# Filler matmuls on constants in five waits of TensorE, in a sliding-window attention kernel followed by a mixture of experts

## The chip, the cores and the metric

The kernel runs on one core of one Trainium2 chip. The metric is the time of one execution on the device in microseconds (us). Before the change it is the median of three runs.

## The reference

Attention over 8 batches, 8 heads, 576 positions and a head size of 64, in which a position sees the positions at a distance of at most 32; then a layer with 8 experts, of which each of the 4608 rows goes to one.

```python
scores = scale * np.matmul(q, k.transpose(0, 1, 3, 2))
mask = np.abs(pos[:, None] - pos[None, :]) <= 32
attn = softmax(np.where(mask, scores, -1e9))
x = np.matmul(attn, v)                       # -> rows of 512 = 8 heads x 64
logits = x @ w_gate + modality_bias[modality_id]
e = argmax(logits); gate = softmax(logits)[e]
out[row] = gate * (relu(x[row] @ w1[e]) @ w2[e])   # 512 -> 1024 -> 512
```

## The kernel before

All work is cut into small named operations, and one long string, `ORDER`, gives the order in which the program issues them. A token is read as a name, its numbers, after a slash the engine that copies (`a` ScalarE or ACT, `v` VectorE or DVE, `p` GpSimd or POOL), and after a colon the PSUM bank or banks into which TensorE writes. Each engine works through its own instructions in this order; semaphores make it wait for what others have to deliver. The eight PSUM banks are handed out by the string alone.

For each batch, `l` loads q or k for four heads, `c` casts them to bf16 (tile `cb`), `TQ` and `TK` transpose them on TensorE (L496), and `tq` and `tk` copy the result to `qT` and `kT`. `lr`, `cr`, `TR` (L508) and `tr` do the same for the last 64 positions. `lv` loads v, and `cv` casts it to `vt`. For batches 1 and 2 the load of v goes to the tile `vb` in another layout, and the matmuls `Y` (L283) bring it into order, with `yy` as the copy.

The attention runs in 32 steps of a batch and a pair of heads. `SA` and `SB` are the scores of key blocks 0 and 1, and of 2 to 4 (L528, two banks each). `sa` and `sb` are their exponentials on ACT (L536, L539) into the tile `pt`. `M` multiplies by the band mask on DVE (L550), `V` multiplies by v (L564, L569), and `v` normalises on DVE (L578, L579). A copy that POOL makes waits for the latest mask multiplication of DVE, by an explicit dependency. `Kd`, once, prepares the bias from the modality ids: a small transpose (L413) and eleven operations on DVE.

After each batch `X` transposes its rows (L590) and `L` computes the logits (L603). The chains `lo`, `B`, `Q` and `E` pick the expert; `R` counts the rows by a triangular matmul (L657, L659); `P` makes each row's place (its last step gives `di`). `Z` scatters the batch's rows by expert into a table in device memory, in five indirect transfers that POOL issues (L690). `F` fetches a tile of 256 rows of the table, `N` transposes it, `U` (L824) and `D` (L842) are the two expert matmuls, `u` and `y` their copies, and `O` scatters the result rows to the output (L859). `W` loads an expert's weights on POOL's queue (L732, L735).

So the first stage, in which the first batches' attention and routing run, has little for TensorE to do and many chains between engines; later, attention and the expert matmuls are interleaved and TensorE has work all the time.

The two constants that the change uses are in place early: `ident` is a 128 x 128 identity, and `mask` the band mask of 128 x 192, written by POOL (L353 to L356) between its first and its second cast.

Of the kernel before, what the change touches and what calls it, by code (L numbers as in the profile page):

```python
# [33 lines left out]
TK1:3 tk0/a TR0:4 tk1/v lv0.1 tr0.0/a SA0:56 lv0.2 tr0.1/a c0.1.0/v sa0 lv0.3 SB0:01 SA1:23 sb0 TQ2:7 SB1:45  # L34
tq2/v c0.1.1/p TQ3:6 lv0.4 sa1 tq3/v TK2:0 sb1 M0 l1.0.0 TK3:1 l1.0.1 Kd:7 tk2/a cv0.0/p lr1.0 tk3/a M1 lr1.1
cv0.1/p l1.1.0 cv0.2/a l1.1.1 V0:23 V1:45 v0 c1.0.0/p zp SA2:01 SB2:67 sa2 v1 SA3:23 sb2 c1.0.1/p SB3:01 TQ4:4
TQ5:5 lv1.0 sa3 tq4/v TK4:6 TK5:7 M2 sb3 lv1.4 tk4/v cr1/p tq5/a V2:23 M3 tk5/a TR1:4 SA4:01 tr1.0/a tr1.1/a
v2 c1.1.0/p V3:56 sa4 c1.1.1/p v3 TQ6:7 SB4:23 TQ7:4 tq6/a W0 SA5:01 sb4 tq7/v X0.0:5 X0.1:6 X0.2:7 x0.0/v
X0.3:4 x0.1/a x0.2/v X0.4:2 Y1.0:3 x0.3/a x0.4/v Y1.1:5 yy1.0/a Y1.2:6 M4 yy1.1/a L0:7 Y1.3:4 yy1.2/a lo0
SB5:23 B0.0 I0 yy1.3/a TK6:5 B0.1 TK7:7 Q0.0 sa5 B0.2 tk6/v E0 B0.3 sb5 V4:01 tk7/v SA6:45 B0.4 Q0.1 SB6:67 v4  # L40
sa6 R0:2 sb6 P0.0 Q0.2 P0.1 P0.4 P0.2 P0.5 P0.3 A0.0 Z0.0 Z0.1 Z0.2 Z0.3 Z0.4 A0.1 M5 l2.0.0 l2.0.1 lr2.0 A0.2
V5:34 M6 lr2.1 SA7:01 l2.1.0 SB7:56 sa7 A0.3 l2.1.1 v5 sb7 V6:01 A0.4 c2.0.0/p v6 F0 TQ8:2 A0.5 TQ9:7 M7 tq8/a
F1 lv2.0 tq9/a l3.0.0 c2.0.1/p V7:34 l3.0.1 v7 lr3.0 lv2.4 cr2/a TK8:5 TK9:6 lr3.1 tk8/a TR2:0 tk9/v X1.0:1
tr2.0/a X1.1:2 X1.2:7 x1.0/a tr2.1/v c2.1.0/p X1.3:3 l3.1.0 X1.4:4 x1.1/v x1.2/a SA8:56 SB8:01 x1.3/a x1.4/v
TQ10:2 TQ11:7 sa8 tq10/v L1:4 sb8 tq11/v SA9:23 SB9:56 lo1 B1.0 I1 sa9 B1.1 Q1.0 Y2.0:7 B1.2 E1 M8 Y2.1:4
yy2.0/a Y2.2:0 yy2.1/a Y2.3:1 B1.3 Q1.1 B1.4 l3.1.1 yy2.2/a Q1.2 R1:2 yy2.3/v c2.1.1/p sb9 N0:3 P1.0 P1.1
TK10:7 P1.2 TK11:4 n0/a P1.4 V8:01 P1.3 P1.5 Z1.0 tk10/v N1:5 tk11/a v8 SA10:23 U0.0:6 n1/a Z1.1 U0.1:7 u0.0/a
Z1.2 c3.0.0/v sa10 SB10:01 u0.1/v U0.2:4 Z1.3 sb10 c3.0.1/v TQ12:5 U0.3:6 Z1.4 u0.2/a tq12/v TK12:2 TQ13:3
u0.3/a W1 A1.0 TK13:7 lv3.0 M9 D0.0.0:0 tk12/a lv3.1 tq13/a lv3.2 D0.0.1 A1.1 M10 tk13/a lv3.3 Ke V9:45 y0.0/a
lv3.4 D0.1.0:1 A1.2 v9 cr3/a c3.1.0/a V10:23 A1.3 i0 SA11:67 TR3:0 A1.4 sa11 SB11:45 v10 F2 O0.0 D0.1.1 sb11  # L50
tr3.0/v l4.0.0 SA12:67 TQ14:2 A1.5 TQ15:3 tr3.1/v c3.1.1/p sa12 tq14/v SB12:45 M11 sb12 TK14:0 TK15:2 tk14/v
tq15/a V11:67 M12 tk15/a SA13:45 l4.0.1 sa13 SB13:23 v11 cv3.0/p sb13 lr4.0 y0.1/v X2.0:0 X2.1:4 X2.2:5 x2.0/a
M13 X2.3:6 F3 X2.4:7 x2.1/a x2.2/a x2.3/v O0.1 lr4.1 x2.4/a i1 L2:2 U1.0:3 lo2 B2.0 I2 B2.1 U1.1:1 Q2.0
cv3.1/p u1.0/a l4.1.0 U1.2:0 E2 u1.1/a B2.2 B2.3 Q2.1 U1.3:4 B2.4 u1.2/a Q2.2 cv3.2/p l4.1.1 R2:5 u1.3/a P2.0
V12:67 P2.1 P2.2 V13:23 P2.4 P2.3 P2.5 SA14:01 Z2.0 v12 N2:4 sa14 v13 n2/a SB14:56 Z2.1 SA15:01 sb14 SB15:23
Z2.2 c4.0.0/v lv4.0 U2.0:7 sa15 Z2.3 TQ16:4 u2.0/v U2.1:5 sb15 A2.0 TQ17:6 M14 U2.2:0 u2.1/a U2.3:1 lv4.1 A2.1
u2.2/a A2.2 tq16/v tq17/a V14:23 u2.3/v D1.0.0:7 Z2.4 c4.0.1/a v14 lv4.2 D1.0.1 A2.3 TK16:5 A2.4 y1.0/a N3:0
M15 TK17:4 n3/a D1.1.0:6 A2.5 lv4.3 tk16/v O1.0 V15:12 tk17/a cr4/v D1.1.1 v15 TR4:3 y1.1/a SA16:45 c4.1.0/p
U3.0:7 tr4.0/v lv4.4 sa16 tr4.1/v O1.1 X3.0:0 X3.1:1 u3.0/v X3.2:2 x3.0/a X3.3:6 X3.4:3 x3.1/v x3.2/a SB16:45
TQ18:7 i2 x3.3/a D2.0.0:0 x3.4/v sb16 c4.1.1/p SA17:12 tq18/v l5.0.0 L3:6 F4 TQ19:3 i3 sa17 U3.1:7 lo3 M16 I3  # L60
tq19/a SB17:45 TK18:6 u3.1/a D2.0.1 B3.0 tk18/v sb17 F5 TK19:1 B3.1 U3.2:2 B3.2 Q3.0 B3.3 E3 tk19/v D2.1.0:3
y2.0/a l5.0.1 u3.2/v U3.3:7 O2.0 cv4.0/a lr5.0 D2.1.1 u3.3/a B3.4 Q3.1 M17 R3:6 lr5.1 D3.0.0:4 y2.1/a l5.1.0
P3.0 D3.0.1 O2.1 cv4.1/a cv4.2/v D3.1.0:5 y3.0/a P3.1 l5.1.1 Q3.2 P3.2 P3.4 V16:01 P3.3 P3.5 Z3.0 c5.0.0/a
V17:23 v16 SA18:67 lv5.0 TQ20:4 sa18 D3.1.1 Z3.1 v17 tq20/a SB18:01 TQ21:6 Z3.2 y3.1/v sb18 N4:7 SA19:23
tq21/v SB19:45 Z3.3 n4/a Z3.4 sa19 U4.0:0 A3.0 sb19 lv5.1 M18 U4.1:1 U4.2:6 u4.0/a A3.1 u4.1/v O3.0 lv5.2
c5.0.1/a V18:23 u4.2/v O3.1 U4.3:7 cr5/a v18 lv5.3 TK20:4 u4.3/a TR5:5 A3.2 TK21:0 tk20/v U5.0:1 tr5.0/a
tr5.1/a lv5.4 A3.3 M19 SA20:23 tk21/a D4.0.0:6 u5.0/a SB20:45 A3.4 sa20 i4 U5.1:7 F6 A3.5 i5 sb20 c5.1.0/p
c5.1.1/v V19:01 D4.0.1 l6.0.0 u5.1/a v19 SA21:23 TQ22:4 sa21 l6.0.1 TK22:5 M20 TQ23:7 SB21:01 tq22/a TK23:2
tk22/v cv5.0/p lr6.0 X4.0:3 sb21 X4.1:4 x4.0/v X4.2:5 x4.1/a lr6.1 x4.2/v X4.3:3 X4.4:0 U5.2:1 x4.3/a M21
x4.4/a l6.1.0 D4.1.0:4 cv5.1/p cv5.2/v u5.2/a l6.1.1 L4:5 tq23/a tk23/v U5.3:3 y4.0/a lo4 B4.0 I4 F7 i6 V20:01  # L70
B4.1 u5.3/a Q4.0 O4.0 V21:56 E4 v20 SA22:23 D4.1.1 sa22 lv6.0 B4.2 Q4.1 SB22:01 B4.3 Q4.2 y4.1/a D5.0.0:7 B4.4
v21 c6.0.0/p sb22 lv6.1 SA23:23 R4:4 D5.0.1 O4.1 c6.0.1/v lv6.2 sa23 SB23:56 P4.0 TQ24:0 M22 sb23 TK24:1 lv6.3
TQ25:2 TK25:3 P4.1 tq24/a P4.2 V22:56 P4.4 lv6.4 tk24/a P4.3 P4.5 U6.0:4 A4.0 Z4.0 v22 tq25/a SA24:01 u6.0/a
U6.1:2 l7.0.0 tk25/v Z4.1 sa24 y5.0/v D5.1.0:5 u6.1/a Z4.2 cr6/v U6.2:6 c6.1.0/a A4.1 TR6:4 M23 U6.3:3 u6.2/a
tr6.0/a TQ26:0 A4.2 u6.3/a D5.1.1 Z4.3 tr6.1/v l7.0.1 tq26/a c6.1.1/v V23:12 Z4.4 y5.1/a SB24:67 v23 TK26:4
sb24 TQ27:3 O5.0 TK27:0 U7.0:5 lr7.0 tk26/v tq27/a O5.1 SA25:12 tk27/v X5.0:6 X5.1:7 u7.0/a lr7.1 X5.2:4
x5.0/v X5.3:3 x5.1/a X5.4:0 D6.0.0:5 A4.3 x5.2/a x5.3/v SB25:67 x5.4/a A4.4 M24 D6.0.1 F8 sa25 L5:3 A4.5 sb25
y6.0/v cv6.0/p U7.1:4 l7.1.0 lo5 D6.1.0:0 O6.0 cv6.1/v l7.1.1 cv6.2/a u7.1/a U7.2:1 B5.0 I5 Q5.0 B5.1 V24:23
E5 M25 lv7.0 u7.2/a U7.3:5 B5.2 Q5.1 V25:67 B5.3 u7.3/a lv7.1 B5.4 D6.1.1 Q5.2 v24 c7.0.0/p c7.0.1/a SA26:45
R5:1 lv7.2 y6.1/a v25 SB26:23 cr7/p lv7.3 sa26 O6.1 TQ28:0 P5.0 SA27:67 sb26 tq28/v SB27:45 P5.1 F9 P5.4  # L80
TK28:0 P5.2 sa27 TR7:1 P5.5 P5.3 TQ29:2 A5.0 TK29:3 M26 sb27 U8.0:6 lv7.4 A5.1 D7.0.0:7 tk28/a tr7.0/v Z5.0
u8.0/v tr7.1/a V26:45 tq29/a tk29/v Z5.1 U8.1:0 c7.1.0/a v26 SA28:12 Z5.2 D7.0.1 u8.1/a c7.1.1/v sa28 SB28:34
Z5.3 TQ30:6 U8.2:5 sb28 y7.0/v Z5.4 tq30/v TK30:0 TQ31:1 u8.2/a TK31:2 tk30/v D7.1.0:7 tq31/a A5.2 M27 tk31/a
U8.3:3 D7.1.1 A5.3 u8.3/a M28 V27:45 y7.1/a A5.4 D8.0.0:6 i7 F10 A5.5 v27 O7.0 cv7.0/a SA29:01 D8.0.1 sa29 i8
F11 SB29:23 O7.1 y8.0/a cv7.1/v X6.0:7 X6.1:4 X6.2:5 x6.0/a X6.3:0 X6.4:1 x6.1/v O8.0 U9.0:6 x6.2/a x6.3/v
x6.4/a D8.1.0:7 i9 u9.0/a cv7.2/p L6:4 sb29 i10 U9.1:5 lo6 B6.0 I6 V28:01 B6.1 u9.1/a Q6.0 B6.2 M29 U9.2:6 E6
SA30:23 U9.3:4 u9.2/a B6.3 B6.4 Q6.1 sa30 v28 R6:5 D8.1.1 u9.3/a P6.0 V29:23 Q6.2 y8.1/a P6.1 P6.4 SB30:01
P6.2 U10.0:6 P6.3 sb30 P6.5 A6.0 v29 Z6.0 SA31:45 D9.0.0:7 u10.0/a SB31:01 sa31 A6.1 U10.1:2 M30 sb31 D9.0.1
u10.1/v Z6.1 V30:34 y9.0/a A6.2 U10.2:6 M31 D9.1.0:5 u10.2/a A6.3 v30 Z6.2 V31:01 U10.3:2 Z6.3 v31 D9.1.1
u10.3/a Z6.4 X7.0:7 X7.1:6 X7.2:3 y9.1/a A6.4 x7.0/v O8.1 X7.3:4 x7.1/a X7.4:0 U11.0:1 x7.2/v x7.3/a O9.0  # L90
D10.0.0:2 u11.0/a x7.4/v F12 U11.1:5 A6.5 i11 O9.1 L7:7 u11.1/a D10.0.1 F13 lo7 B7.0 I7 U11.2:6 B7.1 Q7.0
y10.0/a B7.2 B7.3 D10.1.0:3 E7 B7.4 u11.2/a O10.0 R7:4 U11.3:0 P7.0 P7.1 Q7.1 D10.1.1 P7.2 u11.3/a Q7.2 P7.3
P7.4 i12 D11.0.0:1 y10.1/a P7.5 A7.0 Z7.0 U12.0:5 D11.0.1 u12.0/a A7.1 i13 A7.2 U12.1:7 Z7.1 y11.0/a D11.1.0:2
u12.1/a A7.3 Z7.2 U12.2:6 A7.4 Z7.3 D11.1.1 u12.2/a U12.3:4 A7.5 y11.1/a Z7.4 H0 H1 J0 D12.0.0:0 u12.3/a H2
O10.1 H3 J1 U13.0:3 H4 H5 H6 O11.0 D12.0.1 H7 u13.0/a H8 H9 U13.1:5 O11.1 y12.0/a F14 G0 G1 D12.1.0:1 G2
# [14 lines left out]
def kernel(  # L110
# [12 lines left out]
    nc = tc.nc  # L123
    B, H, S, D = q.shape
    P = 128
# [186 lines left out]
    ident = const.tile([P, P], BF16)  # L312
# [229 lines left out]
    op["SA"] = lambda _, it: scores(it, 0)  # L542
    op["SB"] = lambda _, it: scores(it, 2)
    op["sa"] = lambda _, it: exps(it, 0)
    op["sb"] = lambda _, it: exps(it, 2)

    @named
    def M(_, it):
# [550 lines left out]
```

## Time and profile before

| | before |
|---|---|
| time of three runs | 262.41, 263.61, 263.88 us, median 263.61 |
| profiled execution | span 262.5 us, mean granted TensorE clock 0.946 |
| TensorE busy | 221.5 us (84%), 2529 matmuls |
| ACT, DVE, POOL busy | 170.7, 159.5, 126.0 us (65%, 61%, 48%) |
| data moved | 52.14 MB, mean 199 GB/s |
| chain that ended last | TensorE 42%, issue 15%, POOL 8%, DVE 6%, DMA 3%, ACT 3% |

The profile is of one execution. Busy times are sums over the span and say nothing about when: TensorE's slices show four to seven tenths in the first third and nine tenths afterwards. The granted clock is the share of full speed at which TensorE may run; it has its own row of 40 slices, each 6.6 us long. "Idle before, released by" in the rows below means how long an engine stood still before an instruction, and what ended that.

### The profile page before, as it was taken

Reading aid. Unit: us, or ns where it says so; the run is one execution under the profiler, and the core shown is the slowest. Engines: PE = TensorE matmul, PEld = TensorE weight load, DVE = VectorE, ACT = ScalarE, POOL = GpSimd, SP = SyncE. Lnnn points to the kernel's source line nnn. Section 1 sums busy time; section 2 is a strip of 40 time slices with the busy share of each in tenths; the row PEclk is TensorE's granted clock in tenths of the full one; section 3 lists DMA queues with packets and bytes.
Section 4 is the critical chain, followed back from the end, with each engine's and each line's share of the span. In section 5 each row is a group of like instructions: output and inputs, shape, how many; then the busy total and the mean of one; then the engine's idle time right before and its main releaser. Section 6 shows DMA issues by size and latency. Waiting matters only on the chain.

```text
span 262.5 us, 6727 instructions
## 1 busy us (share of the span) xinstructions
PE 221.5 (84%) x2529; PEld 157.3 (60%) x2529; DVE 159.5 (61%) x463; ACT 170.7 (65%) x296; POOL 126.0 (48%) x162
## 2 busy tenths in 40 slices
PE   0736676298977999998999999999999999999960
PEld 0426535286745876666775777667677666666630
DVE  7684949459788579757887769884863815100000
ACT  2653745279886596879787996978746455555540
POOL 2937512863875275057244755644374671222240
PEclk9999975569998899999999999999999999999996
DMA  4999999599999998999499999949029559422220
GB/s 154 267 224 283 272 259 212 153 167 295 294 182 236 303 303 212 216 310 298 125 245 249 267 289 212 267 123 203 20 80 204 183 167 201 133 81 85 81 82 8
DMA packets 85523, 52.14 MB, mean 199 GB/s; under 512 B 58435, under 2 KB 81003, under 8 KB 85483
## 3 DMA queue, kind: packets, MB, share of 16 engines
q1 hardware_dynamic: 73131, 31.27, 54.2%
q0 software_dynamic: 11680, 19.84, 29.0%
q10 hardware_dynamic: 672, 0.53, 0.6%
q8 instruction: 21, 0.34, 0.6%
q14 instruction: 19, 0.16, 0.2%
HBM read 38.18 MB, written 16.11 MB: 207 GB/s over the span
## 4 chain that ended last, share of the span: by engine, by line
PE 42%; issue 15%; POOL 8%; DVE 6%; DMA 3%; ACT 3%; POOLq 1%; DVEq 0%; ACTq 0%
PE banks L824 15%; PE banks L842 13%; POOL out_dram L859 5%; PE banks L528 3%; DMA out_dram<-ys,ix 3%; PE banks L496 3%; PE banks L590 3%; PE banks L564 2%; ACT pt L536 2%; PE banks L569 2%; POOL scr L690 1%; DVE xt L579 1%; DVE pt L550 1%; PE banks L603 1%; DVE kT L191 1%
## 5 line engine op out<-in xcount | busy, mean ns | idle before, releaser
L824 PE MATMUL banks<-xTf,w 128*128 128x256 bf16 (+1 forms) x608 | 77.2, 273 | 1.0 <-ACT xTf L189 0.9
L842 PE MATMUL banks<-w,hT 128*128 128x512 bf16 x296 | 74.7, 379 | 0.0
L824 PEld LDWEIGHTS <-w 128*128 128x128 bf16 x608 | 56.9, 99 | 15.8 <-issue 1.7
L859 POOL DMA_INDIRECT out_dram<-ys,ix x37 | 37.4, 1011 | 57.4 <-ACT ys L850 31.9
L690 POOL DMA_INDIRECT scr<-xt,di x40 | 44.7, 1118 | 39.0 <-issue 37.0
L835 ACT ACTIVATE hT<-banks 128x512 bf16<-128x512 f32 x65 | 39.0, 599 | 34.8 <-PE banks L824 34.0
L536 ACT ACTIVATE pt<-banks 128x768 bf16<-128x768 f32 x64 | 50.8, 821 | 14.9 <-PE banks L528 12.0
L842 PEld LDWEIGHTS <-hT 128*128 128x128 bf16 x296 | 27.2, 98 | 21.4 <-issue 0.8
L550 DVE TENSOR_TENSOR pt<-pt,mask 128x1920 bf16<-128x1920 bf16 x32 | 38.0, 1189 | 0.3 <-ACT pt L539 0.3
L496 PE MATMUL banks<-ident,cb 128*128 128x128 bf16 x256 | 24.0, 241 | 15.0 <-POOL cb L193 14.7
L564 PE MATMUL banks<-vt,pt 128*128 128x65 bf16 x320 | 24.0, 203 | 9.9 <-POOL vt L193 4.8
L496 PEld LDWEIGHTS <-cb 128*128 128x128 bf16 x256 | 17.7, 108 | 19.9 <-POOL cb L193 16.2
L564 PEld LDWEIGHTS <-pt 128*128 128x128 bf16 x320 | 22.5, 104 | 9.4 <-DVE pt L550 5.0
L579 DVE TENSOR_TENSOR xt<-banks,rec 128x640 bf16<-128x640 f32 x32 | 26.4, 824 | 1.2
L528 PE MATMUL banks<-qT,kT 64*128 64x192 bf16 (+1 forms) x320 | 24.5, 262 | 0.6 <-DVE xt L579 0.3
L193 POOL TENSOR_SCALAR cb<-qkf 128x1024 bf16<-128x1024 f32 x17 | 18.0, 1061 | 14.0 <-PE banks L283 5.1
L569 PE MATMUL banks<-vt,pt 128*128 128x65 bf16 x256 | 23.0, 203 | 0.0
L569 PEld LDWEIGHTS <-pt 128*128 128x128 bf16 x256 | 19.9, 104 | 4.1 <-issue 4.1
L850 ACT ACTIVATE ys<-banks,xm 128x512 f32<-128x512 f32 x24 | 16.5, 688 | 8.2 <-PE banks L842 8.1
L189 ACT COPY qT<-banks 128x512 bf16<-128x512 bf16 (+1 forms) x24 | 13.0, 549 | 11.5 <-PE banks L496 10.4
L528 PEld LDWEIGHTS <-kT 64*128 64x128 bf16 x320 | 12.2, 101 | 12.6 <-issue 9.5
L578 DVE RECIPROCAL rec<-banks 128x10 f32<-128x10 f32 x32 | 6.9, 215 | 16.3 <-PE banks L569 13.1
(182 smaller groups left out, 258.5 us busy)
## 6 DMA issues: line engine op xcount, KB each, us to landing
qkf<-in_q_dram SPq DMA_DIRECT2D x16, 512.0 KB, 7.1
qkf<-in_k_dram SPq DMA_DIRECT2D x15, 512.0 KB, 7.8
vf<-in_v_dram SPq DMA_DIRECT2D x24, 256.0 KB, 6.4
w<-in_moe_w_dram POOLq DMA_DIRECT2D x4, 1024.0 KB, 14.7
xg<-scr SPq DMA_DIRECT2D x5, 272.0 KB, 6.3
rf<-in_q_dram SPq DMA_DIRECT2D x8, 128.0 KB, 12.8
rf<-in_k_dram SPq DMA_DIRECT2D x8, 128.0 KB, 6.7
vb<-in_v_dram POOLq DMA_DIRECT2D x2, 512.0 KB
```

The source lines that it names most:

```text
L496: nc.tensor.transpose(tp[:, i, :], Ct["c", b, hp // 2, u][:, i, D * l_:D * l_ + P], ident[:])
L528: nc.tensor.matmul(st[:, h, c0:c0 + w_], k_t[b % 2][D * h:D * h + D, hp, P * j:P * j + P], q_t[b % 2][D * h:D * h + D, hp, P * j:P * j + w ...
L536: nc.scalar.activation(p_ap, st[:, :, 0:2 * WIN].rearrange("p h (j c) -> p h j c", c=WIN), ACT.Exp, scale=scale)
L550: masked.append(nc.vector.tensor_tensor(out=p_ap, in0=p_ap, in1=mask[:].unsqueeze(1).to_broadcast([P, 2 * NM, WIN]), op=ALU.mult))
L564: nc.tensor.matmul(o_ap, pt[:, h, SW * m:SW * m + P], vt[:, m, 2 * hp + h, :], start=(m == 0), stop=(m == 0), skip_group_check=True)
L569: nc.tensor.matmul(o_ap, pt[:, h, c1:c1 + P], vt[:, m - 1, 2 * hp + h, :], start=False, stop=True, skip_group_check=True)
L579: nc.vector.tensor_tensor(out=x_bf(b)[:, :, P * hp:P * hp + P].rearrange("p m (h d) -> p h m d", h=2), in0=o_v[:, :, :, 0:D], in1=rec[:].u ...
L690: ins = nc.gpsimd.indirect_dma_start(out=scr[:], out_offset=bass.IndirectOffsetOnAxis(ap=Ct["di", b][:, m:m + 1], axis=0), in_=x_t[b % 2][ ...
L824: nc.tensor.matmul(ph[:, u, :], w1_sb[t % 2][:, kd, P * mi:P * mi + P], Ct["N", t][1][:, kd, 0:w_], start=(kd == 0), stop=(kd == n_kd - 1))
L835: nc.scalar.activation(o_ap, Ct["U", t, mp][:], ACT.Relu)
L842: nc.tensor.matmul(Ct["D", t, s], Ct["h", t][:, kf, P * s:P * s + P], w2_sb[t % 2][:, kf, :], start=(kf == 0), stop=(kf == n_kf - 1))
L859: ins = nc.gpsimd.indirect_dma_start(out=out, out_offset=bass.IndirectOffsetOnAxis(ap=Ct["i", t][:, s:s + 1], axis=0), in_=Ct["y", t, s][: ...
```

## The change

A new operation `w` issues a given number of matmuls whose operands are constants: the identity as weights, the mask as moving operand, 192 columns each. Their results are read by nobody. Each group writes into the bank, or the first of the two banks, of the operation that follows it in TensorE's order, which overwrites them. The string gets five such tokens: 16 before `SA0` in bank 5, 16 before `V0` in bank 2, 16 before `V5` in bank 3, 32 before `TQ8` in bank 2, and 8 before `TK14` in bank 0; in all 88 matmuls. It is for keeping TensorE busy where it is known to wait, so that its clock is not lowered, or is raised sooner.

No other token moves; the instructions of DVE, ACT, POOL and the load queues keep their order. The compiled order of TensorE shows that the first group waits for nothing that is not already waited for, and the group before `V0` for an ACT copy that `V0` waited for before. In the diff the string is wrapped anew, so most of its lines differ; here it is cut to the tokens around the five places.

```diff
-TK1:3 tk0/a TR0:4 tk1/v lv0.1 tr0.0/a SA0:56 lv0.2 tr0.1/a c0.1.0/v sa0 lv0.3 SB0:01 SA1:23 sb0 TQ2:7 SB1:45
+TK1:3 tk0/a TR0:4 tk1/v lv0.1 tr0.0/a w16:5 SA0:56 lv0.2 tr0.1/a c0.1.0/v sa0 lv0.3 SB0:01 SA1:23 sb0 TQ2:7
...
-cv0.1/p l1.1.0 cv0.2/a l1.1.1 V0:23 V1:45 v0
+cv0.1/p l1.1.0 cv0.2/a l1.1.1 w16:2 V0:23 V1:45 v0
...
-l2.0.1 lr2.0 A0.2 V5:34 M6 lr2.1 SA7:01 l2.1.0 SB7:56 sa7 A0.3 l2.1.1 v5 sb7 V6:01 A0.4 c2.0.0/p v6 F0 TQ8:2
+l2.0.1 lr2.0 A0.2 w16:3 V5:34 M6 lr2.1 SA7:01 l2.1.0 SB7:56 sa7 A0.3 l2.1.1 v5 sb7 V6:01 A0.4 c2.0.0/p v6 F0 w32:2 TQ8:2
...
-SB12:45 M11 sb12 TK14:0 TK15:2
+SB12:45 M11 sb12 w8:0 TK14:0 TK15:2
...
     @named
+    def w(_, n_):
+
+        for _i in range(n_):
+            nc.tensor.matmul(bank([P, WIN]), ident[:], mask[:], start=True, stop=True)
+
+    @named
     def M(_, it):
```

## The prediction

> **What bounds the kernel now.** I read the page from its second part (the slices), then the windows view in stretches of 4 us, then who waited for whom on TensorE in three stretches, and last the timeline around each of the five places. The windows view splits the run in two:
>
> ```profile
> core 0: us, PE busy (x) PEld busy (x) DVE busy (x) ACT busy (x) POOL busy (x), PEclk, DMA share, GB/s
> 18.00:22.00 4.00, 0.49 (x10) 0.49 (x10) 2.25 (x9) 0.62 (x1) 1.60 (x2) 1.00 1.16 281
> 22.00:26.00 4.00, 3.85 (x55) 3.25 (x53) 2.00 (x5) 2.04 (x4) 3.15 (x4) 1.00 1.14 282
> 34.00:38.00 4.00, 2.87 (x35) 1.43 (x35) 1.69 (x6) 1.57 (x3) 0.00 (x0) 0.76 1.21 290
> 50.00:54.00 4.00, 1.25 (x16) 1.26 (x17) 0.74 (x1) 0.61 (x2) 3.98 (x4) 0.50 0.19 66
> 54.00:58.00 4.00, 4.00 (x57) 3.60 (x55) 2.77 (x6) 3.24 (x7) 2.61 (x4) 0.68 1.17 187
> 82.00:86.00 4.00, 3.51 (x43) 2.69 (x41) 3.32 (x8) 1.96 (x4) 3.47 (x4) 0.73 1.17 246
> 86.00:90.00 4.00, 4.00 (x55) 3.43 (x53) 1.26 (x9) 2.52 (x5) 0.03 (x1) 0.84 1.12 305
> ```
>
> The column PEclk gives the clock's edges. 0.76 over 34 to 38 means half rate from 36.1; 0.68 over 54 to 58 means full rate again from 56.5; 0.73 and 0.84 mean a second half-rate spell from 83.9 to 87.3. The 1.00 before 25.8 is only a missing record: in the timeline the 65-column matmuls of 21.5 to 24 us start 54 ns apart, those of 28 us 30 ns apart, so TensorE ran at half rate from the start to about 25.8.
>
> Before 84 us TensorE mostly waits; the waits view for 0 to 57 us says
>
> ```profile
> PE banks L496 <- POOL cb L193: 13.2, 5, 7.1
> PE banks L564 <- POOL vt L193: 4.8, 2, 4.0
> PE banks L564 <- DVE pt L550: 3.9, 3, 2.4
> PE banks L283 <- DMA vb<-in_v_dram: 1.9, 1, 1.9
> ```
>
> and for 84 to 262 us its four rows add up to only 1.6 us, the largest being
>
> ```profile
> PE banks L824 <- ACT xTf L189: 0.9, 1, 0.9
> ```
>
> So from 84 us on TensorE is the bound, and whatever the start shifts at 84 us shifts the end nearly one for one. Before that the bound is a chain over POOL, DVE, ACT and TensorE, in which TensorE's rate counts only where nobody else ends last.
>
> [...] its edges lie 10.2, 20.5, 27.3 and 3.4 us apart, all multiples of 3.41. I worked out the share of each such window in which columns streamed: 0.81, 0.93 and 0.92 lifted the clock, 0.75 and 0.67 did not; 0.39 and 0.28 dropped it, 0.43 and 0.44 did not. [...] here the window before 56.5 was two thirds transposes and lifted the clock, so I count them. [...]
>
> **The change, part by part.** It adds 88 matmuls of 192 columns and moves nothing else. The rows give 54 ns for 65 columns at half rate, hence 0.160 us for one fill; at full rate 30 ns or less, hence about 0.085. Its weight load (98 to 108 ns in the rows) lies beside the matmul before it.
>
> *w16 before SA0.* 16 x 0.160 = 2.56 us. There is no wait to fill here:
>
> ```profile
> 10.53 0.61 PE L508 MATMUL banks<-ident,rb 128*128 128x128 bf16 x4 [0.20 <-ACT rb L189]
> 11.07 1.42 PE L528 MATMUL banks<-qT,kT 64*128 64x192 bf16 x14
> ```
>
> SA0 followed at once. Queued behind the fill are SA0, SB0, SA1, TQ2, SB1, TQ3; ACT's exps (L536, 11.70), DVE's M0 (14.82), the bias chain, M1 (19.17), POOL's copy of vt (20.40) and V0 (third matmul 21.51) wait for them one after the other. Something comes back: with the fill TensorE streams nearly without a break from 9.29, so the clock can lift somewhere in 12.4 to 15.8 us, and the 2.4 us of work behind the fill would halve. I take +1.6 us at V0; the ends are +1.0 (lifted early, ACT's three exps then bind) and +2.5 (not lifted).
>
> *w16 before V0.* 2.56 us at most, in a wait of 0.79 + 4.03 us for POOL's vt. Hidden; it ends before the copy of vt, and the clock falls in the rest of the wait anyway.
>
> *From V0 to vb.* POOL's third copy after vt had 0.45 us of idle for a load, which eats part of the delay, so vb's load (issued 23.90) starts about 1.15 us later. It landed at 35.13 as the wait of 1.9 us above. I take its landing at +1.0 (ends +0.5, other loads finishing sooner, and +1.8). TensorE itself arrives 1.6 later, so its idle time before L283 falls from 1.9 to about 1.3 us. That matters for the clock: the window of 32.7 to 36.1 was 0.39 busy, and 0.6 us less idle makes it about 0.55, over the level that dropped. So full rate is likely to hold past 36 us.
>
> *36 to 44 us at full rate.* From L283 at 35.13 to DVE's copy of kT (L191, 39.84) it took 4.71 us. At full rate: 1.0 as before, L603 0.5, four 512-column matmuls 0.85 instead of 1.88, SB5 0.33, TK6 0.23, and 0.23 to the copy, together 3.14. DVE is then back to back to di (43.12), and POOL's first scatter (L690, 44.19) follows. So +1.0 - 1.57 = -0.55 us at the scatters; +1.0 if the clock drops all the same.
>
> *w16 before V5, w32 before TQ8.* The first stands in the 2.40 us wait for DVE pt L550 (fill 1.36 to 2.56 us: at most 0.2 late, for V5, which feeds nothing that POOL's five scatters up to 51.6 wait for). The second stands in
>
> ```profile
> 52.75 1.03 PE L496 MATMUL banks<-ident,cb 128*128 128x128 bf16 x8 [4.33 <-POOL cb L193]
> ```
>
> with 2.7 us at full and 5.1 at half rate, so TQ8 is at most 0.6 late, and TK8 (54.78) waits for POOL's copy of 53.63 to 54.72 anyway. So it costs nothing and TensorE meets TK8 warm. Before, 54.78 to 56.54 ran at half rate without a break: 1.76 us become 0.88. ACT was busy 3.24 of these 4 us, so I take -0.7 at SA8 (57.49). It feeds L1's logits, DVE's di, the second five scatters (from 64.2) and by them TK14 and TK15 (77.97).
>
> *w8 before TK14.* 0.68 us in the wait of 1.50 for POOL before 77.97: free. It fills the stretch around 76 to 79, which was under 0.4 busy; but the window 80.4 to 83.8 (0.28 busy) is not touched. The half-rate spell of 83.9 to 87.3 hit 3.1 us of unbroken matmuls, 1.55 us of loss. [...] I give one in three that it is avoided: -0.5.
>
> Sum: -0.55 - 0.7 - 0.5 = -1.75 us, 263.6 - 1.75 = 261.9.
>
> **The rivals.** (1) *The first fill is paid in full.* No wait stands before SA0 (for it); a clock that lifts within the fill speaks against. +2.5 at V0, +1.8 at vb, and if the clock drops at 36 again, -0.4 left of the warm start at TK8: +1.4, 265.0, slower. (2) *Hidden both ways.* vb's landing absorbs the early delay, but the chain over POOL's scatters and ACT absorbs the faster matmuls as well; for it: POOL was 3.98 of 4 us busy over 50 to 54. The delay of 1.0 against 0.5 to 1.0 gained: 263.4. (3) *All half-rate spells after 30 us go.* -0.55 - 0.9 - 1.55 and some 0.5 more at vb: 260.1. Against it: the untouched window of 0.28.
>
> **How the numbers follow.** Forecast 0.44, rival 1 0.22, rival 2 0.24, rival 3 0.10. The forecast's own spread (the spell at 84 us stays or goes, 1.55 us) puts about 0.06 of its 0.44 within 0.5% of before (1.3 us). So faster 0.48, same 0.30, slower 0.22. The range, 259.9 to 265.2, reaches from rival 3 to rival 1 and leaves out about 0.1 on either side: the fill uncompensated down to the end (266) and more than every spell gone.
>
> **What would show it.** Right: SA0 near 13.5, V0's third matmul near 23.1, vb's wait on L283 down to about 1.3 us, PEclk at 1.00 over 37 to 42 and at 54.8, POOL's first scatter near 43.7, TensorE unbroken from about 83 us. Wrong in the first step: V0 not later, or by over 2 us. Wrong in the second: PEclk 0.5 at 38 us though vb's wait shrank, or vb landing as late as TensorE. Wrong in the third: SA8 no nearer to TK8 than before, with ACT ending last. The forecast as a whole fails if the scatters start later than 44.2 us.

## The result and the profile after

In one comparison the changed kernel took 261.27 us (median of 6 runs, 260.49 to 262.08) and the kernel before 263.23 us (6 runs, 262.41 to 263.88): a ratio of 0.9925, with a 95% interval of 0.9897 to 0.9954. Two later comparisons of the same two kernels, with 14 and 23 runs of the changed one, gave 0.9994 [0.9964, 1.0023] and 1.0012 [0.999, 1.0035]. So two questions stand: where the 2 us came from in the first, and why they did not come again. The ratios leave out runs that lie over 1.5% above the fastest of their kernel, which the medians and ranges count; the traces of `e3`, `f2` and `g1` below are of such runs and are read for places, not for times.

The page after has a span of 260.5 us (before 262.5), a mean granted clock of 0.965 (0.946), 2591 matmul records (2529; 88 matmuls were added, so some records are missing) and TensorE busy for 223.7 us (221.5). Both means of the clock count the time before the first clock record as full rate, up to 25.8 us before and 13.5 us after. The windows view of the changed kernel, with the stretches that were shown of before and the one from 38 to 42 us:

```profile
core 0: us, PE busy (x) PEld busy (x) DVE busy (x) ACT busy (x) POOL busy (x), PEclk, DMA share, GB/s
18.00:22.00 4.00, 1.38 (x19) 1.29 (x17) 3.67 (x12) 1.12 (x3) 0.70 (x2) 1.00 1.17 285
22.00:26.00 4.00, 2.81 (x51) 2.44 (x52) 2.00 (x4) 1.07 (x2) 4.00 (x5) 0.72 1.12 287
34.00:38.00 4.00, 3.40 (x48) 1.78 (x46) 2.65 (x8) 2.76 (x7) 0.49 (x2) 0.92 1.25 290
38.00:42.00 4.00, 4.00 (x56) 3.60 (x56) 3.32 (x15) 3.43 (x8) 0.00 (x0) 0.65 1.12 216
50.00:54.00 4.00, 3.02 (x39) 2.86 (x40) 1.24 (x3) 2.18 (x4) 4.00 (x5) 0.63 0.42 76
54.00:58.00 4.00, 3.73 (x74) 3.29 (x76) 3.16 (x8) 3.73 (x8) 0.58 (x2) 0.94 1.33 255
82.00:86.00 4.00, 3.99 (x26) 3.03 (x27) 2.42 (x9) 1.17 (x3) 2.03 (x4) 0.60 1.16 272
86.00:90.00 4.00, 4.00 (x76) 3.28 (x74) 2.44 (x10) 2.46 (x5) 0.92 (x1) 1.00 1.13 321
```

PEclk is again the column to read. Of 34 to 38 us only the last 0.6 is at half rate now (0.92, before 0.76). But 0.65 over 38 to 42, 0.63 over 50 to 54 and 0.60 over 82 to 86 say that three half-rate spells remain, each of 3.4 us: 37.4 to 40.8, 51.0 to 54.5 and 81.8 to 85.2. A fourth, from 23.7 to 27.1, is the 0.72 over 22 to 26. The 20 us at half rate of before (36.1 to 56.5) became two times 3.4. The edges of the clock lie 10.24, 3.41, 10.24, 3.41, 10.24, 3.41, 27.31 and 3.41 us apart here, again whole multiples of 3.41; a window, below, is a stretch of 3.41 us on the grid of these edges.

Who TensorE waited for, 0 to 57 us (waits view, changed kernel; in total, times, longest):

```profile
PE banks L497 <- POOL cb L194: 11.1, 5, 7.2
PE banks L571 <- POOL vt L194: 3.6, 1, 3.6
PE banks L571 <- DVE pt L557: 2.4, 3, 1.1
PE banks L284 <- DMA vb<-in_v_dram: 0.6, 1, 0.6
```

The wait for `vb` went from 1.9 to 0.6 us. TensorE's timeline of the changed kernel around the first fill (L552; the lines of the code up to L529 stand one further down than before, those after the new function seven):

```profile
start us, us, engine line op out<-in xcount [idle before <-releaser]
10.69 0.61 PE L509 MATMUL banks<-ident,rb 128*128 128x128 bf16 x4 [0.20 <-ACT rb L190]
11.09 2.65 PE L552 MATMUL banks<-mask,ident 128*128 128x192 bf16 x16
13.68 0.72 PE L529 MATMUL banks<-qT,kT 64*128 64x192 bf16 x14
...
23.03 0.19 PE L571 MATMUL banks<-vt,pt 128*128 128x65 bf16 x1 [3.64 <-POOL vt L194]
```

SA0 starts at 13.68 instead of 11.07, its 14 matmuls take 0.72 instead of 1.42 us because the clock rose at 13.5, and V0's third matmul starts at 23.03 instead of 21.51.

Where the time of these two executions comes from, read off the timelines (the traced runs took 264.11 us before and 262.08 after, the latter the longest of its six):

| point | before, us | after, us | shift |
|---|---|---|---|
| first scores, SA0 | 11.07 | 13.68 | +2.61 |
| V0's third matmul | 21.51 | 23.03 | +1.52 |
| POOL issues the load of `vb` | 23.90 | 24.93 | +1.03 |
| first matmul on `vb` | 35.13 | 34.85 | -0.28 |
| DVE copies batch 1's first kT | 39.84 | 38.65 | -1.19 |
| first scatter of batch 0 | 44.19 | 42.97 | -1.22 |
| POOL's copy after the fifth scatter | 51.61 | 49.57 | -2.04 |
| first exponential of SA8 | 58.14 | 56.08 | -2.06 |
| first expert matmul of tile 1 | 84.15 | 82.14 | -2.01 |
| end | 262.51 | 260.48 | -2.03 |

Three steps make it: the load of `vb` came early though it was issued late; 0.9 us were won up to DVE's copy of kT, at full rate until 37.4; 0.8 us were won within the five scatters. After 50 us nothing more was gained or lost.

The 0.8 us come from a place that nobody aimed at. The timeline of POOL and DVE, before:

```profile
48.53 0.22 DVE L578 RECIPROCAL rec<-banks 128x10 f32<-128x10 f32 x1 [1.46 <-PE banks L569]
...
49.59 1.15 DVE L550 TENSOR_TENSOR pt<-pt,mask 128x1920 bf16<-128x1920 bf16 x1
49.81 1.78 POOL L690 DMA_INDIRECT scr<-xt,di  x1 [0.30 <-issue]
51.61 1.08 POOL L193 TENSOR_SCALAR cb<-qkf 128x1024 bf16<-128x1024 f32 x1
```

and after:

```profile
46.24 0.22 DVE L585 RECIPROCAL rec<-banks 128x10 f32<-128x10 f32 x1 [0.55 <-PE banks L576]
...
47.30 0.98 POOL L697 DMA_INDIRECT scr<-xt,di  x1 [0.30 <-issue]
47.30 1.19 DVE L557 TENSOR_TENSOR pt<-pt,mask 128x1920 bf16<-128x1920 bf16 x1
48.59 0.98 POOL L697 DMA_INDIRECT scr<-xt,di  x1 [0.30 <-issue]
49.57 1.08 POOL L194 TENSOR_SCALAR cb<-qkf 128x1024 bf16<-128x1024 f32 x1
```

The fifth scatter took 1.78 us where it began 0.22 us after the mask multiplication M7 had begun, and 0.98 us where M7 had begun with the fourth. The long scatter ends 0.85 us after M7 (50.74). It is not chance: in the 14 traces of this document 105 scatters began 0.05 to 1.14 us into such a multiplication, and each ended 0.84 to 0.97 us after it. Why a scatter is late there, no trace shows. The other way round M7 was not held up: it began with or just after a scatter in the trace above and in `e1` (below), and took 1.19 and 1.16 us, hardly more than its usual 1.15. M7 is queued on DVE behind `v6`, whose reciprocal waits for V6: 1.46 us before, 0.55 after. So M7 moved by 2.3 us and the scatters by 1.2, since V5, SA7, SB7 and V6 now ran at full rate. It is argued, not shown, that the fill before V5 kept the clock up: its 1.48 us are about 0.4 of the 0.56 that the window from 40.8 to 44.2 us was busy. In `e3`, which lacks this fill, the clock had dropped earlier already, at 39.3.

### The profile page after: what moved, and what is told of

It is laid out like the page before. It is cut to its first block, busy times and chain, and to the rows that moved or that the text cites. A ratio compares the mean times of both kernels' runs of the same rounds, so it can differ in the third digit from the quotient of the medians.

```text
span 260.5 us, 6877 instructions
## 1 busy us (share of the span) xinstructions
PE 223.7 (86%) x2591; PEld 162.4 (62%) x2617; DVE 159.6 (61%) x463; ACT 170.8 (66%) x296; POOL 125.3 (48%) x162
## 4 chain that ended last, share of the span: by engine, by line
PE 47%; issue 14%; POOL 6%; DVE 6%; ACT 3%; POOLq 1%; DVEq 0%; ACTq 0%
PE banks L831 18%; PE banks L849 14%; POOL out_dram L866 5%; PE banks L529 4%; PE banks L497 3%; PE banks L571 2%; PE banks L597 2%; DVE pt L557 2%; PE banks L576 2%; DVE xt L586 2%; ACT pt L537 1%; POOL cb L194 1%; PE banks L610 1%; ACT xTr L190 1%; DVE rb L192 1%
## 5 line engine op out<-in xcount | busy, mean ns | idle before, releaser
L849 PE MATMUL banks<-w,hT 128*128 128x512 bf16 x270 | 71.2, 379 | 1.7 <-issue 0.5
L697 POOL DMA_INDIRECT scr<-xt,di x40 | 44.0, 1101 | 36.7 <-issue 35.0
L497 PE MATMUL banks<-ident,cb 128*128 128x128 bf16 x256 | 23.1, 235 | 12.4 <-POOL cb L194 11.8
L571 PE MATMUL banks<-vt,pt 128*128 128x65 bf16 x320 | 22.5, 198 | 7.4 <-POOL vt L194 3.6
L497 PEld LDWEIGHTS <-cb 128*128 128x128 bf16 x256 | 17.1, 105 | 17.0 <-POOL cb L194 13.1
L571 PEld LDWEIGHTS <-pt 128*128 128x128 bf16 x320 | 21.0, 100 | 7.4 <-DVE pt L557 3.6
L529 PE MATMUL banks<-qT,kT 64*128 64x192 bf16 (+1 forms) x320 | 23.5, 252 | 0.6 <-DVE xt L586 0.3
L576 PE MATMUL banks<-vt,pt 128*128 128x65 bf16 x256 | 21.6, 198 | 0.0
L576 PEld LDWEIGHTS <-pt 128*128 128x128 bf16 x256 | 18.7, 100 | 3.7 <-issue 3.7
L529 PEld LDWEIGHTS <-kT 64*128 64x128 bf16 x320 | 11.7, 98 | 11.9 <-issue 9.2
```

Source lines behind the costliest of these rows:

```text
L497: nc.tensor.transpose(tp[:, i, :], Ct["c", b, hp // 2, u][:, i, D * l_:D * l_ + P], ident[:])
L529: nc.tensor.matmul(st[:, h, c0:c0 + w_], k_t[b % 2][D * h:D * h + D, hp, P * j:P * j + P], q_t[b % 2][D * h:D * h + D, hp, P * j:P * j + w ...
L571: nc.tensor.matmul(o_ap, pt[:, h, SW * m:SW * m + P], vt[:, m, 2 * hp + h, :], start=(m == 0), stop=(m == 0), skip_group_check=True)
L576: nc.tensor.matmul(o_ap, pt[:, h, c1:c1 + P], vt[:, m - 1, 2 * hp + h, :], start=False, stop=True, skip_group_check=True)
L697: ins = nc.gpsimd.indirect_dma_start(out=scr[:], out_offset=bass.IndirectOffsetOnAxis(ap=Ct["di", b][:, m:m + 1], axis=0), in_=x_t[b % 2][ ...
L849: nc.tensor.matmul(Ct["D", t, s], Ct["h", t][:, kf, P * s:P * s + P], w2_sb[t % 2][:, kf, :], start=(kf == 0), stop=(kf == n_kf - 1))
```

## The experiments

Two theories of the gain stood against each other. One: the early fill lifts the clock in time and is part of the gain. The other: the early fill is a price, paid through the load of `vb`, and the later fills alone bring the gain. Beside them stood the mask multiplication in the way of the scatter, the clock at TK8, and the spell near 84 us. The first four kernels ran on a chip on which the kernel before takes 286.46 us, so they are compared with that alone; its runs scatter widely there (282.58 to 297.63 us), and the times that were expected of the four, of about 262 us, are not those of this chip. "Fills" are the tokens of `w`.

| kernel | fills | median, us (runs) | before, us | ratio |
|---|---|---|---|---|
| `e1` | first only | 287.73 (6) | 286.46 | 1.0116 [1.0035, 1.0197] |
| `e2` | all but the first | 286.56 (22) | 286.46 | 0.9989 [0.9944, 1.0034] |
| `e3` | all but the one before V5 | 289.02 (22) | 286.46 | 1.0048 [1.0006, 1.0091] |
| `e4` | before V0 and TK14 only | 286.39 (22) | 286.46 | 1.0014 [0.998, 1.0049] |
| `f1` | the change | 263.65 (14) | 263.38 | 0.9994 [0.9964, 1.0023] |
| `f2` | all but the first | 262.72 (22) | 263.38 | 0.9969 [0.9947, 0.999] |
| `f3` | where the clock drops | 261.29 (8) | 263.38 | 0.9913 [0.988, 0.9946] |
| `f4` | `f3`, and 48 early ones | 261.15 (11) | 263.38 | 0.9914 [0.9884, 0.9943] |
| `g1` | the change | 263.45 (23) | 262.89 | 1.0012 [0.999, 1.0035] |
| `g2` | first only | 265.68 (6) | 262.89 | 1.0103 [1.0052, 1.0154] |
| `g3` | `f3`, and the first | 262.63 (22) | 262.89 | 1.0009 [0.9983, 1.0035] |
| `g4` | `f3` without its last three | 262.12 (22) | 262.89 | 0.9982 [0.9959, 1.0004] |

### What the first fill costs

`e1` and `g2` keep the first fill alone; `e2` and `f2` leave out nothing but it.

```diff
 (e1, g2: the other four tokens out)
-l1.1.1 w16:2 V0:23
+l1.1.1 V0:23
...
 (e2, f2)
-tr0.0/a w16:5 SA0:56
+tr0.0/a SA0:56
```

> Only the 16 fills before SA0. Theory A (the first fill's delay is swallowed by the wait for vb and it brings nothing itself; the gain sits in the fills before V5 and TQ8): same as before, 263.0 to 263.6, first POOL scatter between 43.5 and 44.5. Theory B (the first fill shortens TensorE's idle time before vb, so the clock holds past 36 us, and that is most of the gain): 261.8 to 262.3, first scatter near 43.0. Theory C (the first fill is a pure cost that the others pay back): 264 or more.

> All fills but the 16 before SA0. Theory A: as good as the change, 261.0 to 261.5, V0's third matmul back near 21.5. Theory B: little gain, 262.3 or more, first scatter at 44. Theory C: better than the change, under 260.8.

> All fills but the 16 before SA0, again beside the change itself. Theory C (the first fill is a pure cost of 0 to 2 us, by vb's landing): 0.3 to 1.5 us faster than the change. Theory B (the first fill shortens the idle time before vb and so holds the clock): 0.5 us or more slower than the change. Theory A: within 0.3 us of the change.

> Only the first fill (16 before SA0). The theory that this fill is a cost (V0 1.5 us later, vb landing late on some executions, the half-rate stretch from about 36 us as long as before): slower than before by 0.5 to 2.5 us, ratio 1.002 to 1.010. The rival, that it brings the early clock lift and with it part of the gain: ratio 0.993 to 0.998 and the first scatter before 43.5 us.

By the ratios the first fill alone is 1% slower than no fill on both chips, with intervals that exclude 1: 2.8 us in `g2` (265.68 against 262.89), which is a little more than was expected. `e1` says less, with six runs against widely scattered ones: its medians differ by 1.3 us. Without the first fill the other four are level with before on one chip and 0.3% faster on the other. Beside the change itself, in the same comparison, leaving it out (`f2` against `f1`) brought 0.9 us by the medians, within theory C, but the two intervals overlap. So the first fill is a price, not a part of the gain. The waits view of `g2` shows that none of the waits shown of before has shrunk by more than 0.3 us:

```profile
PE banks L497 <- POOL cb L194: 14.7, 4, 8.3
PE banks L571 <- POOL vt L194: 4.9, 2, 4.1
PE banks L571 <- DVE pt L557: 3.9, 3, 2.4
PE banks L284 <- DMA vb<-in_v_dram: 1.6, 1, 1.6
```

TensorE had been at full rate from 14.7 to 21.6 us, fell back in the wait for `vt` all the same, and from 38.6 to 59.1 us ran at half rate as before. Its first scatter is at 46.53 us.

`g3` puts the first fill into `f3`, the best version of these (below).

> The version with fills where the clock drops (ratio 0.9913 before), and the first fill put back. If the first fill is a cost: 0.5 to 2 us slower than that version, so ratio 0.993 to 0.999. If it is neutral: 0.990 to 0.993, with V0 1.5 us later and the first scatter nonetheless near 43.4 us.

Its ratio is 1.0009 where `f3` had 0.9913: by the difference 1% or 2.5 us for this fill again, more than expected. The two stand in different comparisons, though, and in that of `g3` a second variant, `g4` (below), came out 0.7% above `f3` as well; so a part of the 1% may lie in the comparison.

The way of the cost can be followed through all traces. From the small transpose L509 ahead of SA0 to M0 it takes 5.3 to 6.0 us in the seven executions with the first fill and 4.1 to 4.3 us in the seven without (means 5.67 and 4.23); to POOL's issue of `vb` 13.9 to 14.6 and 12.7 to 13.4 us. The first matmul on `vb` then starts at 34.85 to 39.07 us with it, 36.95 on the mean, and at 34.84 to 35.74 without, 35.24 on the mean. Counted from L509 the means are 25.27 and 23.81, so 1.5 us of the 1.7 are the fill's; from issue to use the load took 11.0 us on the mean with it and 10.9 without. (In `f3`, `f4` and `g3` TensorE came to `vb` straight from another fill, without a wait, so there the load may have ended sooner.) The profiled pair at the top is the lowest of the first group against one of the second.

### The change again

> The change itself once more, beside the kernel before. Theory F (its gain is the clock's state at the few places that end last): ratio 0.990 to 0.995 where the kernel before takes about 263 us. If instead the first fill's delay reaches vb's landing, as it did in the two runs with that fill on the slower chip (vb at 37.3 and 37.8 us against 34.9 and 35.3 in the two without it): 1.000 to 1.008.

> The change itself once more, beside three variants, because its ratio was 0.9925 once and 0.9994 once. If the gain of its first comparison is the rule: ratio 0.990 to 0.995. If the second is: 0.997 to 1.001. Two populations of times within one kernel would show as a wide spread of its runs, 262 to 268 us.

Neither repeats the gain. The execution that was profiled in `f1` has a span of 260.4 us and the same path as at the top (first scatter 43.20, expert matmul of tile 1 at 82.24 us), but the runs reach from 262.05 to 268.58 us. That run took 262.08 us and is the second fastest of its 14; one of the same time was the longest of the six at the top. What made the other five faster, 260.49 to 261.77 us, no trace shows. The one profiled in `g1` is the longest of its 23, 268.0 us. Three rows of its timeline, and one of its waits view:

```profile
12.66 2.77 PE L552 MATMUL banks<-mask,ident 128*128 128x192 bf16 x16
15.36 1.21 PE L529 MATMUL banks<-qT,kT 64*128 64x192 bf16 x14
...
26.86 0.99 POOL L260 DMA_DIRECT2D vb<-in_v_dram  x1
```

```profile
PE banks L284 <- DMA vb<-in_v_dram: 3.4, 1, 3.4
```

The clock rose only at 16.4 us, so that SA0 took 1.21 instead of 0.72 us; the load of `vb` was issued at 26.86 and took 12.2 us to its use instead of 9.9. With `vb` 4.2 us later, the first scatter was at 48.10 and the first expert matmul of tile 1 at 87.72 us, 5.6 later than in the trace at the top. So in the three traces of the change the one with the late `vb` is the bad one. That it comes late is not confined to so long a run: in `e1` and `g2` it was first used at 37.79 and 37.50 us. Why the load takes 9.9 us in one and 12.2 in another was not settled: the DMA engines were busy throughout (shares of 1.09 and more), with loads of q and k beside it.

### The fill before V5 and the scatter

`e3` leaves out the fill before V5; `e4` has only those before V0 and TK14.

```diff
-lr2.0 A0.2 w16:3 V5:34
+lr2.0 A0.2 V5:34
```

> All fills but the 16 before V5. Theory D (that fill makes V5, SA7, SB7 and V6 run at full rate, so that DVE's next mask multiplication is over before POOL's fifth scatter starts and doesn't hold it up): 0.6 to 0.9 us slower than the change, about 262.0, the fifth scatter taking 1.8 us again instead of 0.98. Rival E (the fifth scatter's length has another cause, or the fill before TQ8 warms TensorE as well alone): 261.3, fifth scatter 0.98.

> Only the 16 fills before V0 and the 8 before TK14. All theories but one: the same as before, 263.0 to 263.5, since the first stands in a wait of 4 us and the second doesn't touch the window of 80 to 84 us. The forecast's step for the 8 fills (one in three that the half-rate spell at 84 us is avoided): 262.7, PEclk at 1.00 over 82 to 86 in one run out of three.

Theory D failed: both had a fifth scatter of 0.98 us, though without this fill: M7 began at 53.46 (`e3`) and 50.53 us (`e4`), 2.0 us after the scatter. So the fill before V5 is not needed to avoid the meeting; it needs M7 to be either well before or after. `g2`, with the first fill alone, had the meeting as before:

```profile
51.93 1.15 DVE L557 TENSOR_TENSOR pt<-pt,mask 128x1920 bf16<-128x1920 bf16 x1
52.16 1.78 POOL L697 DMA_INDIRECT scr<-xt,di  x1 [0.30 <-issue]
```

and `e1`, in which the scatter was the first by 0.03 us, did not:

```profile
53.04 0.98 POOL L697 DMA_INDIRECT scr<-xt,di  x1 [0.30 <-issue]
53.07 1.16 DVE L557 TENSOR_TENSOR pt<-pt,mask 128x1920 bf16<-128x1920 bf16 x1
```

In `f3` and `f2` the fifth scatter began later into M7, after 0.84 and 1.00 us, and took 1.17 and 1.00. Together they show that it matters which of the two begins first (1.78 against 0.98 us for the scatter); they show also that 0.8 us of a kernel's time can hang on a meeting of two instructions within a quarter of a microsecond. As a test of the fill before V5 the ratio of `e3` says little, since the change itself was not run on that chip. `e4` was the same as before, as expected of all theories but one, and kept its half-rate spell, from 83.4 to 86.8 us.

### Fills where the clock drops

To say which fill is too small, I took it that a window's share of busy time sets the clock of the next, which is a reading of the traces, and worked out for each trace what share of each 3.41 us window TensorE streamed columns, and beside it the same with each matmul counted by its rows of 128. The list has windows with `Y`'s matmuls in them, whose operands have 32 rows:

```
kernel   window, us      by columns   by rows as well   clock
before   36.1 to 39.5    0.75         0.40              stays half
e1       38.1 to 41.5    0.82         0.39              stays half
g1       40.3 to 43.7    0.83         0.48              stays half
g2       38.6 to 42.0    0.81         0.45              stays half
after    34.0 to 37.4    0.56         0.30              drops
g4       35.9 to 39.3    0.57         0.35              drops
f1       34.2 to 37.6    0.58         0.41              stays full
f2       34.9 to 38.3    0.69         0.44              stays full
```

By rows, the windows of all 14 traces between 3 and 230 us fall into place but for two narrow bands: 63 windows that lifted the clock were busy by 0.72 or more and 65 that left it at half rate by 0.77 or less; 50 that dropped it by 0.39 or less and 740 that kept it by 0.37 or more. By columns the list contradicts such levels: 0.83 does not lift and 0.57 drops, where other windows lift from 0.71 and keep from 0.38. That these matmuls count by about a quarter is an estimate that fits these shares; it was not measured by itself.

`f3` therefore leaves out the first fill, sets 16 full-height matmuls before `Y1.0`, lengthens the one before TQ8 to 40, and adds 12 before `X2.0` and 8 before `L2` for the spell near 84 us. `f4` adds to it 48 matmuls of 128 columns before TQ0, an early lift that stands before nothing that is ready. `g4` is `f3` without the fills before TK14, X2.0 and L2.

```diff
-w16:5 SA0:56
+SA0:56
...
-X0.4:2 Y1.0:3
+X0.4:2 w16:3 Y1.0:3
...
-w32:2 TQ8:2
+w40:2 TQ8:2
...
-y0.1/v X2.0:0
+y0.1/v w12:0 X2.0:0
...
-L2:2 U1.0:3
+w8:2 L2:2 U1.0:3
```

> Without the first fill, with 40 instead of 32 before TQ8, and three groups more in the windows whose drop the traces show: 16 before Y1.0 (bank 3), 12 before X2.0 (bank 0), 8 before L2 (bank 2). Theory F (what counts is the clock at Y1, at TK8 and at 82 to 87 us): 1.5 to 3 us faster than the change, PEclk at 1.00 from 28 us on, SA8's exponentials within 6.0 us of POOL's copy for TQ8. Rival G (the gain comes from other causes, and more fills only delay): within 0.5 us of the run without the first fill, or slower.

> The same, and 48 matmuls of identity by identity (128 columns) in bank 0 before TQ0, in the 5 us in which TensorE waits for the first load. They raise the clock before the first transposes without standing between two links. Theory F: M0 up to 0.9 us earlier, 0.3 to 0.9 us faster than the run before it. Rival H (the clock falls again by the sparse work of 7 to 20 us, or ACT's exponentials end last there): no difference, within 0.3 us.

> The version with fills where the clock drops, without its last three fills (8 before TK14, 12 before X2.0, 8 before L2), so that only the stretch up to TQ8 is filled. If those three take away the half-rate spell near 82 to 87 us: the spell is back in this execution and the time is 0.8 to 1.5 us above that version, ratio 0.994 to 0.997. If full rate up to 57 us was what brought the gain: ratio 0.990 to 0.993, spell or no spell.

`f3` is 2.1 us faster than before in its comparison, and faster than the change beside it (0.9913 [0.988, 0.9946] against 0.9994 [0.9964, 1.0023]), within the range of theory F. Against `f2`, which lacks the first fill too, it gained 1.4 us by the medians, so most of it comes from the added fills. This stands on 8 runs, and 11 of `f4`, in one comparison. Its windows:

```profile
34.00:38.00 4.00, 4.00 (x61) 2.81 (x58) 2.51 (x7) 2.12 (x5) 0.52 (x2) 1.00 1.24 307
38.00:42.00 4.00, 3.49 (x62) 2.78 (x61) 3.17 (x14) 3.99 (x8) 0.00 (x0) 1.00 1.12 215
50.00:54.00 4.00, 3.14 (x55) 2.84 (x53) 1.05 (x3) 1.82 (x4) 3.98 (x6) 1.00 0.36 91
54.00:58.00 4.00, 3.38 (x72) 2.94 (x69) 3.49 (x10) 4.00 (x9) 1.18 (x2) 1.00 1.31 226
82.00:86.00 4.00, 3.94 (x52) 3.48 (x48) 2.43 (x11) 2.43 (x6) 2.07 (x3) 1.00 1.18 241
86.00:90.00 4.00, 3.31 (x74) 2.70 (x71) 3.02 (x10) 2.14 (x4) 1.97 (x3) 1.00 1.08 372
```

All six at 1.00. The clock is still at half rate from 21.8 to 32.0 and from 45.6 to 49.1 us, where theory F wanted it full from 28 on, and full from there to 257 us. From POOL's copy after the scatters to SA8's exponentials it takes 5.77 us, where before and after took 6.53 and 6.51: that is the warm TK8. `f2` and `f4`, full there too, took 5.77 and 5.78, and `g1`, `g2` and `g4`, with half rate in that stretch, 6.90, 6.59 and 6.92.

`f4` does not differ from `f3`: with the clock lifted at 6.1 us, SA0 is at 12.31 and the load of `vb` is issued at 24.65, against 12.15 and 24.42. The lift did not last: the clock fell again at 9.5 us, before SA0, and rose at 19.7, as rival H had it. So what an early lift that holds would bring was not tested.

`g4` came out at 0.9982, slower than both expectations. By the difference to `f3` the last three fills are worth 1.8 us, but the two stand in different comparisons, and the execution of `g4` that was profiled had no half-rate spell near 84 us at all (the window from 80.3 to 83.7 was 0.41 busy and kept the clock), while TK8 fell into one from 53.0 to 56.4. The clock had dropped at 39.3 too: the 16 fills before `Y1.0` had ended at 35.3 in this execution, before the window from 35.9 to 39.3 began. So what these three fills bring by themselves is not settled.

## Why the prediction was right, and where not

The forecast was -1.75 us and the comparison gave -1.96 (263.23 to 261.27), with the profiled spans at -2.03. The direction and the size hold for that comparison. Three of its terms do not, and that they offset one another is luck.

- *The fill before SA0.* SA0 near 13.5 was 13.68, V0's +1.6 was +1.52, and the lift within the fill was at 13.5. Right. The fill before V0 ran in the wait for `vt`, and cost nothing.
- *`vb`'s landing, +1.0.* This is the term that was mis-sized, and the one on which the result turns: -0.28 in this execution, though the load was issued 1.03 later, about as reckoned (1.15); +1.7 by the means of seven traces with the first fill and seven without. In a run like the former the kernel gains 2 us; in one like `g1` it loses 4.
- *The clock holds past 36 us.* It dropped at 37.4. The window's share was foreseen at about 0.55 and is 0.56 by columns, but 0.30 if rows count. That step took 32-row matmuls at full weight, which is what fits its failure; in the kernel before the same count had 0.75 as a window that did not lift, where by rows it is 0.40. Still the half rate lasted one window in place of six, so the stretch to DVE's copy of kT gained 0.91 of the 1.57 us. With `vb` early, the first scatter moved -1.22 in place of -0.55 (the prediction's own +1.0 - 1.57 is -0.57).
- *TK8 warm, -0.7.* Zero here. The fill before TQ8 ended near 48.7 us, TensorE then stood idle for 1.94, the window was 0.37 busy and the clock dropped at 51.0. The size was right where it held: `f3` gained 0.76 in that stretch. In its place the fifth scatter brought -0.8, which the prediction had not named. It had said that V5 feeds nothing which the five scatters wait for. No semaphore does; but V6 behind it sets, by `v6` on DVE, when M7 runs, and M7 stood in the fifth scatter's way.
- *The spell near 84 us, -0.5 on the mean.* It stayed, at 81.8 to 85.2. The prediction's odds of one in three were its author's estimate.
- *From 84 us on the shift carries.* -2.01 there, -2.03 at the end. Right.

Of the rivals, the second, hidden both ways at 263.4, has the number of the later comparisons (263.65 and 263.45 us), but not the mechanism: the early delay is not absorbed where `vb` lands, it is passed on there. The first, the fill paid in full, is what `g2` shows of that fill alone (265.68). So what was right in the first comparison was the sum. As the mean of this change over many runs, about no change has more evidence: 37 runs in two comparisons against 6 in one. What made the first comparison better was not found: its two traces reach L509 at 10.53 and 10.69 us and all later ones at 11.36 to 12.26, with or without fills, so they started about a microsecond sooner; why is not known, nor on which chip they ran.

## What to carry to other kernels

In this kernel filler matmuls paid inside a wait, and where the window in which the clock would drop got them; ahead of a matmul that was ready, as the first fill, they were paid at half rate (2.65 us for 16), and the delay travelled on by a load that was issued later. Here the shares by rows sorted the windows (raised from 0.72, dropped up to 0.39) and those by columns did not (0.83 not raised, 0.57 dropped), so reckon a window's share both ways before saying that a fill is large enough. Where one load's landing decides the path, repeat the comparison on its own, since six runs that agree within 0.6% were followed by 37 with another mean.

## What the runs showed of the hardware

- The clock's edges lay whole multiples of 3.41 us apart (10.24, 20.48, 27.31 and 3.41 us before; 10.24, 3.41 and 27.31 after). By rows, the 50 windows of the 14 traces that dropped the clock were busy by up to 0.39, and the 63 that raised it by 0.72 or more.
- Matmuls on 32 rows seem to count for the clock about as their share of the 128 rows, an estimate: a window that streamed 0.83 by columns and 0.48 by rows did not raise it (`g1`), and one of 0.57 and 0.35 dropped it (`g4`). No run isolates this.
- Indirect scatters of POOL that began within a mask multiplication of DVE ended 0.84 to 0.97 us after it, 105 times in the 14 traces, and took up to 1.96 us (1.78 in the kernel before and in `g2`). One that began first, by 0.03 us in `e1`, took 0.98, and the multiplication 1.16.
- The kernel before took 286.46 us on one chip, and 263.38 and 262.89 on another.
